# Attention feeding a mixture of experts: the first x sums moved into the last attention batch

## The chip, the cores and the metric

The kernel runs on one core of a Trainium2 chip, as one program. The metric is the time of one execution on the device in microseconds (us); the time before is 684.04 us, the median of three runs from 683.57 to 684.36. The core has five engines that run side by side, each through its own list of instructions in order: PE (TensorE, matrix products; PEld is its weight load), DVE (VectorE), ACT (ScalarE), POOL (GpSimd) and SP (SyncE, which here only issues DMAs). An instruction starts when the one in front of it on its engine is done and when the semaphores it waits for are set.

## What is computed

The output of an attention over sorted blocks is the input of a mixture of eight experts. Cut to what matters here:

```
# attention: batch 4, 8 heads, 768 tokens, head size 64, 8 blocks of 96 tokens
P = five rounds of exp and row and column normalisation of sort_net      # 8 x 8 per head
k_s, v_s = P mixes the blocks of k and of v
x = softmax(q_block . k_s_block / 8) . v_s_block       # -> 3072 tokens x 512

# experts
P = exp(x @ w_gate - max)                              # 3072 x 8
for _ in range(8):
    P /= P.sum(1) + 1e-9; P /= P.sum(0) + 1e-9; P *= 3072 / 8
out = sum over e of P[:, e] * (relu(x @ w1[e]) @ w2[e])     # w1: 512 x 1024, w2: 1024 x 512
```

The largest entry of the logits is taken over all tokens, and the columns of P are summed over all tokens, so the routing can't start before the attention of the last batch is done.

## The kernel before, in words

**Attention.** The four batches follow each other. Batch 0 runs alone; beside batches 1, 2 and 3 the kernel weaves expert 0 of the batch before (`weave`, L371 to L408; `expert`, L294 to L311). For a pair of heads the steps are: `queries` (transposes), `keys` (L188, sorted keys; DVE copies them out of PSUM as kTs, L201), `scores` (L207, products L215 and Exp on ACT), `mix` (L225, products with the values L232; DVE takes reciprocals, L235, and scales, L236, into og), `turn` (L240, transposes L243 and a copy into xtT, L246). xtT holds x with the 512 features on partitions, as four blocks of 128, for all 3072 tokens. `logits` gives L257 and glog (L261). Expert 0 gives L299 and L306 on PE, relu on ACT (L301) and a copy to osbl on DVE or ACT (L314). In this part PE's results go to eight PSUM banks in turn: PE can write a bank again only when the result that lay in it eight turns before has been read.

Under batch 3 POOL loads w1 of expert 1 (L84), makes its eight sums (`sum_w`, L332), and issues the load of w2 of expert 1 (L89).

**Sums for fewer products.** Experts 1 to 7 multiply 2 x 2 blocks with seven products in place of eight (a Strassen form). That needs sums of blocks of each operand: of w1 (`sum_w`), of w2 (`sum_w2`, L449, eight per expert), of x (`sum_x`, L454 to L460, four per 1024 tokens p = 0, 1, 2; three into xc, one in place into xtT), and of the hidden layer (L570, L620). The four x sums of p = 0 need the tokens of batches 0 and 1 alone. All run on POOL, but the x sums of p = 0 and p = 2, which run on DVE.

**SBUF.** The pools of the attention are closed at L410, and the later pools take their place in the order in which they are opened (L415, L416): mpc, xcp (xc), wq and wcq (weights), htp, fsp, hsp, w2q. A later tile waits for the last use of the attention tiles whose place it takes.

**Routing and the seam.** `balance` (L467 to L502) is a chain of small steps: the largest logit (L475, matmul L476, L478), its negative on all partitions (matmul L480, L482 gneg), Exp on ACT (L483), then eight iterations of three thirds: L489 to L491 on DVE (row sums), L493 and L494 on DVE (scale, column sums), and matmul L496 on PE with L497, L499 and L500 on DVE. Each next step hangs on the one in front. Expert 0 of batch 3 (`last_dense`, L669 to L700) is 28 steps of PE: 16 of four matmuls of 128x384 (L687, with a relu on ACT behind each) and 12 of four matmuls of 128x512, half an output tile each (L695, with a copy on ACT behind each second). An order written out by hand, L702 to L704, weaves 13 of these (T), seven steps of the chain (C) and the four x sums (X).

**Rounds.** From L726 a loop of rounds r follows. A round of an expert has seven PE steps p1, p5, p6, p2, p7, p3, p4 (two matmuls of 128x512 each, L519); ACT copies or applies relu behind p1, p5, p6, p2 and p4 (L539, L554, L548, L505); DVE adds and applies relu behind p7 and p3 (L508). Five banks go round: p5 writes the bank that p4 of the round before filled and ACT's relu reads; p4 writes a bank that L508 behind p7 reads. In the first five rounds (r < 5) the loop puts expert 0's last 15 steps between them (`outs`, L746 to L748) and the rest of the chain (L767 to L769). From r = 5 on the rounds carry the output products (L630) of the round five before, and DVE gathers them into osbl (L580).

Nearly all of this is pinned: PE and POOL run in the order of the text. The instructions that are not pinned (the memset and copy at L463 and L465, L314) may be placed among the others by the scheduler.

Of the kernel before, what the change touches and what calls it, by code (L numbers as in the profile page):

```python
# [14 lines left out]
BF16 = mybir.dt.bfloat16  # L15
AF = mybir.ActivationFunctionType
AX = mybir.AxisListType
ALU = mybir.AluOpType


def mkap(t, dims, off=0):
    return bass.AP(tensor=t.tensor, offset=t.offset + off, ap=dims)
# [3 lines left out]
def kernel(  # L26
# [11 lines left out]
    nc = tc.nc  # L38
# [25 lines left out]
    pin = tc.keep_in_program_order  # L64
# [27 lines left out]
    Ibig = ones.tile([128, 128], BF16)  # L92
# [287 lines left out]
    with ExitStack() as c2:  # L380
# [31 lines left out]

    late = lambda name, bufs: ctx.enter_context(
        tc.tile_pool(name=name, bufs=bufs, reuse_waits="tile"))
    mpc, xcp, wq, wcq = late("mpc", 1), late("xcp", 1), late("wq", 2), late("wcq", 1)  # L415
    htp, fsp, hsp, w2q = late("htp", 1), late("fsp", 1), late("hsp", 3), late("w2q", 1)  # L416
    banks = lambda name, bufs: tc.tile_pool(name=name, bufs=bufs, space=bass.MemoryType.PSUM,
                                            reuse_waits="tile")
    load_w2(1)
# [31 lines left out]

    xc = xcp.tile([128, 3, 2, N // 2], BF16)

    def sum_x(p, eng):  # L454
        ta, tb = (slice(1024 * p + 512 * i, 1024 * p + 512 * i + 512) for i in range(2))
        b11, b12, b21, b22 = (xtT[:, k:k + 2, t] for k in (0, 2) for t in (ta, tb))
        x1, x2, x4 = (xc[:, j, :, 512 * p:512 * p + 512] for j in range(3))
        for a, b, c in ((b12, b11, x1), (b22, x1, x2), (b22, b12, b12), (b21, x2, x4)):
            pin(eng.tensor_tensor(out=c, in0=a, in1=b, op=ALU.subtract))
            yield  # L460

    onesc = mpc.tile([128, 128], F32)
    nc.vector.memset(onesc, 1.0)  # L463
    I128 = mpc.tile([128, 128], F32)
    nc.vector.tensor_copy(I128, Ibig)  # L465

    def balance():  # L467

        room = rings["oacc"][2]
        G = room[:, 0:NT * E].rearrange("p (t e) -> p t e", e=E)  # L470
        sums = room[:, 192:192 + NT]
        csps = room[:, 256:256 + E]
        gmps = room[:, 384:512]
        gm = mpc.tile([128, 1], F32)
        pin(nc.vector.reduce_max(out=gm, in_=glog.rearrange("p t e -> p (t e)"), axis=AX.X))  # L475
        pin(nc.tensor.matmul(gmps[0:1, :], gm, I128, start=True, stop=True))  # L476
        gm1 = mpc.tile([1, 1], F32)
        pin(nc.vector.reduce_max(out=gm1, in_=gmps[0:1, :], axis=AX.X, negate=True))  # L478
        yield
        pin(nc.tensor.matmul(csps[:, 0:1], onesc[0:1, :], gm1, start=True, stop=True))  # L480
        gneg = mpc.tile([128, 1], F32)
        pin(nc.vector.tensor_copy(gneg, csps[:, 0:1]))  # L482
        pin(nc.scalar.activation(out=G, in_=glog, func=AF.Exp, bias=gneg))  # L483
        rs2 = mpc.tile([128, NT], F32)
        cs2 = mpc.tile([128, E], F32)
        cs1 = mpc.tile([128, E], F32)
        yield
        for it in range(8):
            pin(nc.vector.reduce_sum(out=sums, in_=G, axis=AX.X))  # L489
            pin(nc.vector.tensor_scalar_add(rs2, sums, 1e-9))  # L490
            pin(nc.vector.reciprocal(out=rs2, in_=rs2))  # L491
            yield
            pin(nc.vector.tensor_mul(G, G, mkap(rs2, [rs2.ap[0], rs2.ap[1], [0, E]])))  # L493
            pin(nc.vector.reduce_sum(out=cs2, in_=G.rearrange("p t e -> p e t"), axis=AX.X))  # L494
            yield
            pin(nc.tensor.matmul(csps, onesc, cs2, start=True, stop=True))  # L496
            pin(nc.vector.tensor_scalar(out=cs1, in0=csps, scalar1=float(E) / N,  # L497
                                        scalar2=1e-9 * E / N, op0=ALU.mult, op1=ALU.add))
            pin(nc.vector.reciprocal(out=cs1, in_=cs1))  # L499
            pin(nc.vector.tensor_mul(glog if it == 7 else G, G,  # L500
                                     mkap(cs1, [cs1.ap[0], [0, NT], cs1.ap[1]])))
            yield  # L502
# [166 lines left out]
    def last_dense():  # L669

        at = [0]

        def two_banks():
            at[0] += 1
            return rings["oacc"][at[0] % 2]

        for c in range(2):
            c0 = (B - 1) * S + c * 384
            if c == 0:
                h = [hTb[1][:, fb, 0:384] for fb in range(8)]  # L680
            else:
                two = [hsp.tile([128, 4, 384], BF16, name="hs") for _ in range(2)]
                h = [two[fb // 4][:, fb % 4, :] for fb in range(8)]
            for fb in range(8):
                hps = (rings["bk"][(0, 2, 3)[fb % 3]] if c == 0 else two_banks())[:, 0:384]
                for kk in range(4):
                    pin(nc.tensor.matmul(hps, w1t[0][:, kk, fb * 128:(fb + 1) * 128],  # L687
                                         xtT[:, kk, c0:c0 + 384],
                                         start=(kk == 0), stop=(kk == 3)))
                pin(relu(h[fb], hps))  # L690
                yield
            for tt in range(3):
                oacc = rings["bk"][(1, 4)[tt]] if c == 0 and tt < 2 else two_banks()
                for fb in range(8):
                    pin(nc.tensor.matmul(oacc, h[fb][:, tt * 128:(tt + 1) * 128],  # L695
                                         w2t[0][:, fb, :], start=(fb == 0), stop=(fb == 7)))
                    if fb == 3:
                        yield
                pin(nc.scalar.copy(osbl[:, c0 // 128 + tt, :], oacc))
                yield  # L700

    dense, chain, xs = last_dense(), balance(), sum_x(0, nc.vector)  # L702
    for step in "TTCXTTXCXXTTCCTTTCCTTCTT":
        next({"T": dense, "C": chain, "X": xs}[step])  # L704

    queue = [sum_w2(1), sum_x(1, nc.gpsimd)]

    def weights(n):
# [6 lines left out]
    C = 3 * (E - 1)  # L715
# [4 lines left out]
    for m, o in enumerate(ends):  # L720
        e, p, hT, _ = chunks[-1]
        for j in range(2):
            spares += plain(e, p, 4 * j + o.i, hT, bank, 2 if m == 1 and j == 1 else 1)
    late, before = None, None
    weights(8)
    for r in range(len(pairs) + 6):  # L726
        n, i = r // 4, r % 4
        if n < C:
            e, p, hT, s3 = chunks[n]
            if i == 0 and (n == 1 or n > 1 and p == 0) and e + 1 < E:  # L730
                load_w1(e + 1)
                queue.append(sum_w(e + 1))
            if r == 8 or p == 1 and i == 2 and n > 1 and e + 1 < E:
                load_w2(2 if r == 8 else e + 1)
                queue.append(sum_w2(2 if r == 8 else e + 1))
            steps, rest = hidden(e, p, i, hT, s3, r < 4)
        else:
            steps, spares, rest = spares[:7], spares[7:], None
        if r == 5:
            xs = sum_x(2, nc.vector)  # L740
        k = r - 5
        if k + 1 in range(len(pairs)):
            pairs[k + 1].sums()
        weights((0, 2, 2, 0, 0)[r] if r < 5 else 4 if r < 8 else 1 + i % 2)
        now = pairs[k] if k in range(len(pairs)) else None
        if r < 5:  # L746
            outs = [None, lambda: next(dense), None, lambda: next(dense), None,
                    lambda: next(dense)]  # L748
        else:
            outs = [getattr(a, b) for a, b in  # L750
                    ((now, "q5"), (before, "q7"), (now, "q1"), (before, "q4"),
                     (now, "q6"), (now, "q2"), (now, "q3")) if a]
        if r == 5:
            for _ in chain:
                pass
            scale0([0, 4])
        for j in range(max(len(steps), len(outs))):
            if j < len(steps):
                steps[j]()
                if j == 3 and n < C:  # L760
                    if k + 1 in range(1, 12):
                        scale0([8 * ((k + 1) // 4) + (k + 1) % 4 + 4 * m for m in range(2)])
                    if k + 1 in range(len(pairs)):
                        pairs[k + 1].keep()
            if j < len(outs) and outs[j]:
                outs[j]()
            if r < 5 and j in (0, 1, 3, 4, 5):  # L767
                if (5 * r + (0, 1, 0, 2, 3, 4)[j]) % 4 != 3:
                    next(chain, 0)  # L769
            if j == 1 and late:  # L770
                late()
                late = None
            if j == 3:
                next(xs, 0)
        late, before = rest, now
        if n >= C and not spares and not before:
            break
# [30 lines left out]
```

## Time and profile before

| | |
|---|---|
| runs | 683.57, 684.04, 684.36 us |
| profiled execution, its own time | 683.67 us |
| its span, first to last instruction | 681.9 us |
| granted clock of PE, mean | 0.999 |
| PE busy in 130 to 140 and in 140 to 150 us | 9.32 and 7.13 of 10 |
| PE busy in 240 to 300 us | 59.58 of 60 |
| first L687 step of the seam | 134.44 us |
| first L519 step (round 0) | 148.87 us |
| first step of round 5 | 177.83 us |
| one x sum (128x1024) on DVE | 0.68 to 1.66 us |
| one x sum on POOL | 2.12 us |
| one w1 or w2 sum (128x512) on POOL | 1.14 to 1.61 us |
| w2 load of an expert (1 MB), issue to landing | 9.0 us |

The profile is one execution. A row of a timeline has the start in us, the time in us, the engine, the line, the operation, what is written and read with its size, how many instructions were merged, and in square brackets how long the engine was idle in front and what ended that. Matmuls are pipelined and their ends are modelled: two rows of PE can overlap, and the distance from one start to the next tells more than the time of one. A row of the waits has the engine, the tile and line that waited, what it waited for, the sum, how often, and the longest.

### The profile page before, as it was taken

How to read it: one execution, taken by the hardware profiler on the slowest of the kernel's cores; microseconds unless marked ns; L12 is line 12 of the kernel's file. 1: busy time of each engine (PE TensorE's matmuls, PEld its weight loads, DVE VectorE, ACT ScalarE, POOL GpSimd, SP SyncE). 2: the span in 40 equal slices, each digit the busy share in tenths (PEclk: the TensorE clock that was granted, in tenths of full speed). 3: DMA queues.
4: the chain of work that ended last, by engine and by line, in shares of the span. 5: the costliest groups of instructions: out<-in, count | busy, mean ns of one | idle time of the engine just before them, and what ended most of it. 6: DMA issues, size and time to landing. Idle time of an engine off the chain costs nothing.

```text
span 681.9 us, 13271 instructions
## 1 busy us (share of the span) xinstructions
PE 655.4 (96%) x5058; PEld 434.1 (64%) x5136; DVE 475.6 (70%) x979; ACT 379.6 (56%) x736; POOL 473.8 (69%) x437
## 2 busy tenths in 40 slices
PE   5989999989999999999999999999999999999997
PEld 2646666544566666666666666666666666666665
DVE  6627555676687777777777777777777777777775
ACT  3746646347677765555555555555555555555540
POOL 4542323574888998949698987879796979836641
PEclk9999999999999999999999999999999999999999
DMA  9898843400221304030303021030403040000224
GB/s 147 161 214 131 136 87 63 62 1 10 53 46 18 62 1 63 1 62 1 62 2 58 4 39 26 4 59 1 62 1 62 1 62 1 1 0 32 93 81 169
DMA packets 31905, 36.58 MB, mean 54 GB/s; under 512 B 2016, under 2 KB 24288, under 8 KB 31840
## 3 DMA queue, kind: packets, MB, share of 16 engines
q0 software_dynamic: 26400, 27.82, 25.3%
q1 hardware_dynamic: 5440, 7.90, 3.4%
q8 instruction: 40, 0.66, 0.4%
q14 instruction: 25, 0.20, 0.1%
HBM read 52.45 MB, written 6.29 MB: 86 GB/s over the span
## 4 chain that ended last, share of the span: by engine, by line
PE 82%; DMA 7%; POOL 5%; DVE 4%; issue 1%; ACT 1%; SPq 0%; DVEq 0%; POOLq 0%; ACTq 0%
PE oacc L630 34%; PE bk L519 32%; PE bank L306 4%; PE bank L299 4%; DMA qt<-in_q_dram 3%; POOL hs L620 3%; DMA w2e<-in_moe_w_dram 1%; PE bank L232 1%; DMA w1e<-in_moe_w_dram 1%; PE bk L596 1%; POOL wc L332 1%; PE oacc L695 1%; DMA vsb<-vs 1%; PE bank L215 1%; PE oacc L687 1%
## 5 line engine op out<-in xcount | busy, mean ns | idle before, releaser
L580 DVE SCALAR_TENSOR_TENSOR osbl<-oacc,glog,osbl 128x256 f32<-128x256 f32 (+1 forms) x410 | 219.3, 535 | 127.3 <-PE oacc L630 117.2
L505 ACT ACTIVATE hT<-bk 128x512 bf16<-128x512 f32 (+1 forms) x176 | 104.1, 593 | 148.0 <-PE bk L519 129.8
L519 PE MATMUL bk<-xtT,w1e 128*128 128x512 bf16 x478 | 144.3, 379 | 0.9
L630 PEld LDWEIGHTS <-hs 128*128 128x128 bf16 x984 | 96.2, 98 | 63.0 <-issue 0.3
L630 PEld LDWEIGHTS <-hT 128*128 128x128 bf16 x904 | 88.4, 98 | 59.6 <-issue 2.4
L620 POOL TENSOR_TENSOR hs<-hT 128x512 bf16<-128x512 bf16 x82 | 94.8, 1157 | 37.7 <-DVE hT L508 32.3
L630 PE MATMUL oacc<-w2e,hT 128*128 128x256 bf16 x764 | 114.6, 273 | 1.6 <-DVE osbl L580 1.1
L620 POOL TENSOR_TENSOR hs<-hT,hs 128x512 bf16<-128x512 bf16 x82 | 95.2, 1161 | 6.4
L620 POOL TENSOR_TENSOR hs<-hs,hT 128x512 bf16<-128x512 bf16 x82 | 95.2, 1161 | 6.4
L519 PE MATMUL bk<-xc,wc 128*128 128x512 bf16 x316 | 95.6, 379 | 0.9 <-ACT hT L505 0.8
L630 PE MATMUL oacc<-w2e,hs 128*128 128x256 bf16 x616 | 92.4, 273 | 0.7
L519 PEld LDWEIGHTS <-w1e 128*128 128x128 bf16 x672 | 65.8, 98 | 12.8 <-issue 1.4
L508 DVE CUSTOM_DVE_ANT_0 hT<-bk,p 128x512 bf16<-128x512 f32 x84 | 58.1, 691 | 9.3 <-PE bk L519 1.8
L554 ACT COPY p<-bk 128x512 f32<-128x512 f32 x84 | 49.2, 586 | 24.0 <-PE bk L519 21.3
L548 ACT COPY u<-bk 128x512 f32<-128x512 f32 x84 | 49.3, 586 | 23.0 <-PE bk L519 20.3
L539 ACT COPY bk<-bk 128x512 f32<-128x512 f32 x84 | 48.0, 571 | 20.5 <-PE bk L519 20.5
L508 DVE CUSTOM_DVE_ANT_0 hT<-bk,u 128x512 bf16<-128x512 f32 x84 | 57.1, 680 | 0.0
L630 PE MATMUL oacc<-w2s,hs 128*128 128x256 bf16 x368 | 55.2, 273 | 0.3
L519 PEld LDWEIGHTS <-wc 128*128 128x128 bf16 x504 | 49.3, 98 | 9.2 <-issue 1.6
L573 DVE SCALAR_TENSOR_TENSOR s<-bk,hT 128x512 bf16<-128x512 f32 x80 | 54.5, 681 | 0.0
L519 PE MATMUL bk<-xtT,wc 128*128 128x512 bf16 x160 | 48.2, 379 | 0.4
L519 PE MATMUL bk<-xc,w1e 128*128 128x512 bf16 x159 | 48.0, 379 | 0.4 <-DVE hT L508 0.3
(128 smaller groups left out, 857.0 us busy)
## 6 DMA issues: line engine op xcount, KB each, us to landing
w1e<-in_moe_w_dram POOLq DMA_DIRECT2D x8, 1024.0 KB, 8.1
w2e<-in_moe_w_dram POOLq DMA_DIRECT2D x8, 1024.0 KB, 9.0
out_dram<-osbl SPq DMA_DIRECT2D x23, 256.0 KB, 2.0
vt<-in_v_dram POOLq DMA_DIRECT2D x3, 768.0 KB, 10.8
vsb<-vs SPq DMA_DIRECT2D x16, 97.5 KB, 5.2
vsb<-vs POOLq DMA_DIRECT2D x16, 97.5 KB, 5.2
qt<-in_q_dram POOLq DMA_DIRECT2D x4, 384.0 KB, 13.2
kt<-in_k_dram POOLq DMA_DIRECT2D x4, 384.0 KB, 13.8
```

Source lines behind the costliest of these rows:

```text
L299: hold(nc.tensor.matmul(hps[:, 0:n], w1t[e][:, kk, fb * 128:(fb + 1) * 128], xtT[:, kk, c0:c0 + n], start=(kk == 0), stop=(kk == 3)))
L306: hold(nc.tensor.matmul(oacc, hTs[:, fb, tt * 128:(tt + 1) * 128], w2t[e][:, fb, :], start=(fb == 0), stop=(fb == 7)))
L505: relu = lambda o, x: nc.scalar.activation(out=o, in_=x, func=AF.Relu)
L508: return nc.vector._custom_dve(TENSOR_ADD_SAT, out=o, in0=x, in1=y, s0=TOP, s1=0.0)
L519: pin(nc.tensor.matmul(ps, wa[:, kk, :], xa[:, kk, :], start=(first and kk == 0), stop=(kk == 1), skip_group_check=True))
L539: pin(nc.scalar.copy(t["w"], t["u"]))
L548: pin(nc.scalar.copy(t["u2"], t["u"]))
L554: pin(nc.scalar.copy(t["p5"], t["v"]))
L573: pin(nc.vector.scalar_tensor_tensor(out=s3[:, i, :], in0=t["w"], scalar=0.0, in1=c12, op0=ALU.max, op1=ALU.subtract))
L580: pin(nc.vector.scalar_tensor_tensor(out=o, in0=ps, scalar=glog[:, t, e:e + 1], in1=o, op0=ALU.mult, op1=ALU.add))
L620: pin(nc.gpsimd.tensor_tensor(out=s[:, c], in0=a, in1=b, op=o))
L630: pin(nc.tensor.matmul(ps, h[:, fb, :], w[:, fb, :], start=(first and fb == 0), stop=(fb == 3), skip_group_check=True))
```

## The change

The four x sums of p = 0 are moved from the seam to where the later pools are opened, without being pinned, so the scheduler may place them as soon as their tiles allow. The pools fsp and hsp are opened first, which puts xc over the key and value buffers of the attention. `sum_x` takes the function that pins as an argument.

A tiny copy on POOL, first_x, reads the last of these sums, and it is pinned in POOL's order after the w1 sums; since the load of w2 of expert 1 (`load_w2(1)`) and its sums stand behind it on POOL, these come after the x sums. In the built order DVE has three x sums right after the last kTs copy of batch 3, in front of an osbl copy (L314) and of the mix of the second head pair, and the fourth after the next osbl copy; POOL has memset, first_x, the w2 load, then the w2 sums, then its own x sums for p = 1, as before.

The memset of onesc goes from DVE to POOL and the copy I128 from DVE to ACT. In the built order DVE's L475 stands right behind glog and in front of the last osbl copy.

The order of the seam has the same 13 T and seven C: T stands in pairs between the C's at first. In the rounds r < 5 expert 0's steps stand after p1, p6 and p7 in place of p5, p2 and p3, and a third of the chain is issued in three of each four of all six places, where before it was three of four in five places. The 19 thirds that are left end with the first place of round 4.

```diff
@@ -412,8 +412,9 @@
+    hsp, fsp = late("hsp", 3), late("fsp", 1)
     mpc, xcp, wq, wcq = late("mpc", 1), late("xcp", 1), late("wq", 2), late("wcq", 1)
-    htp, fsp, hsp, w2q = late("htp", 1), late("fsp", 1), late("hsp", 3), late("w2q", 1)
+    htp, w2q = late("htp", 1), late("w2q", 1)
@@ -451,18 +452,22 @@
-    def sum_x(p, eng):
+    def sum_x(p, eng, hold=pin):
...
-            pin(eng.tensor_tensor(out=c, in0=a, in1=b, op=ALU.subtract))
+            hold(eng.tensor_tensor(out=c, in0=a, in1=b, op=ALU.subtract))
...
-    nc.vector.memset(onesc, 1.0)
+    nc.gpsimd.memset(onesc, 1.0)
     I128 = mpc.tile([128, 128], F32)
-    nc.vector.tensor_copy(I128, Ibig)
+    nc.scalar.copy(I128, Ibig)
+    for _ in sum_x(0, nc.vector, lambda ins: ins):
+        pass
+    first_x = mpc.tile([128, 2], BF16)
+    pin(nc.gpsimd.tensor_copy(first_x, xc[:, 2, 0, 0:2]))
@@ -699,9 +704,9 @@
-    dense, chain, xs = last_dense(), balance(), sum_x(0, nc.vector)
-    for step in "TTCXTTXCXXTTCCTTTCCTTCTT":
-        next({"T": dense, "C": chain, "X": xs}[step])
+    dense, chain, xs = last_dense(), balance(), iter(())
+    for step in "TTCTTCTTCCTTCCTTTCTT":
+        next({"T": dense, "C": chain}[step])
@@ -744,7 +749,7 @@
-            outs = [None, lambda: next(dense), None, lambda: next(dense), None,
+            outs = [lambda: next(dense), None, lambda: next(dense), None,
                     lambda: next(dense)]
@@ -764,9 +769,8 @@
-            if r < 5 and j in (0, 1, 3, 4, 5):
-                if (5 * r + (0, 1, 0, 2, 3, 4)[j]) % 4 != 3:
-                    next(chain, 0)
+            if r < 5 and j < 6 and (6 * r + j) % 4 != 3:
+                next(chain, 0)
```

## Prediction

> **What bounds the kernel now.** I read the page's busy times first, then the waits of PE, then the timelines of PE, DVE and POOL around the change, and for the changed program the built order of each engine's instructions with the semaphores they wait for. Lines are those of the kernel before (behind L457 the changed file counts five more).
>
> ```profile
> PE 655.4 (96%) x5058; PEld 434.1 (64%) x5136; DVE 475.6 (70%) x979; ACT 379.6 (56%) x736; POOL 473.8 (69%) x437
> ```
>
> PE is the bound: it is idle for 26.5 us in all. What a change between the attention and the experts can win is PE time at that seam. PE's waits between 136 and 146 us:
>
> ```profile
> PE oacc L496 <- DVE cs L494: 2.1, 1, 2.1
> PE bk L687 <- ACT hT L505: 0.7, 1, 0.7
> PE oacc L476 <- DVE gm L475: 0.6, 1, 0.6
> ```
>
> The same in PE's timeline; L687 and L695 are expert 0's last steps, L476, L480 and L496 the routing's matmuls, 148.87 the first of expert 1:
>
> ```profile
> 136.54 0.38 PE L476 MATMUL oacc<-I,gm 128*1 128x128 f32 x2 [0.63 <-DVE gm L475]
> ...
> 141.43 0.81 PE L687 MATMUL bk<-xtT,w1e 128*128 128x384 bf16 x4 [0.74 <-ACT hT L505]
> ...
> 145.18 0.39 PE L496 MATMUL oacc<-cs,onesc 128*128 128x8 f32 x2 [2.08 <-DVE cs L494]
> ...
> 148.87 0.59 PE L519 MATMUL bk<-xtT,w1e 128*128 128x512 bf16 x2
> ```
>
> DVE shows why: four x sums (L459) lie among the routing's small steps; gneg waits behind two, the first third (L489) behind four.
>
> ```profile
> 137.16 1.66 DVE L459 TENSOR_TENSOR xc<-xtT 128x1024 bf16<-128x1024 bf16 x1
> 138.85 1.53 DVE L459 TENSOR_TENSOR xc<-xtT,xc 128x1024 bf16<-128x1024 bf16 x1
> 140.31 0.14 DVE L482 COPY gneg<-oacc 128x1 f32<-128x1 f32 x1
> 140.37 1.56 DVE L459 TENSOR_TENSOR xtT<-xtT 128x1024 bf16<-128x1024 bf16 x1
> 141.86 1.64 DVE L459 TENSOR_TENSOR xc<-xtT,xc 128x1024 bf16<-128x1024 bf16 x1
> 143.42 0.35 DVE L489 TENSOR_REDUCE oacc<-oacc 128x24 f32<-128x192 f32 x1
> ```
>
> POOL runs its w2 sums beside them; alone one takes 1.15:
>
> ```profile
> 137.12 1.15 POOL L449 TENSOR_TENSOR w2s<-w2e,w2s 128x512 bf16<-128x512 bf16 x1
> 138.23 1.60 POOL L449 TENSOR_TENSOR w2s<-w2e 128x512 bf16<-128x512 bf16 x1
> ```
>
> The two take turns: each x sum ends some 0.55 after a POOL sum does, each POOL sum about 1.0 after an x sum. One that starts just as a POOL sum ends takes 0.68 (195.32 us), and it is the next POOL sum that stretches, to 1.63. Three in a row cost 141.93 - 137.16 = 4.77.
>
> **The change, part by part.**
>
> *Seam: what goes.* From starts, not modelled ends: L687's eight matmuls take 1.30, so L476 could have started at 135.74 and lost 0.80; L480 lost 0.10 (138.15 to 138.25); the last L687 step 0.93 (140.50 to 141.43); L496 2.24 (142.94 to 145.18). Sum 4.07: without waits expert 1 starts at 144.80. Do other waits come instead? In the new order gm stands right behind glog on DVE (133.57), the memset goes to POOL, the I128 copy (0.74 on DVE) to ACT, where 1.82 us lie idle at 114 us; gm is there by 133.95, L476 needs it at 135.74. gm1 (0.41 behind L476) is ready by 136.45, its matmul stands two steps later, at 137.35. gneg follows at 137.9, Exp (0.42) ends at 138.46, the first thirds (0.95 for L489 to L491, 0.76 for L493 and L494) end at 140.2; PE has eight steps done by then, at 140.25. No wait is left: gain 4.07.
>
> *Attention: what comes.* The new layout puts xc over key and value buffers; the program's semaphores ask only for loads long landed and for ACT's xtT copies of batches 0 and 1. So sums 1 to 3 start as soon as DVE has copied the last keys (kTs, 116.72), and stand in front of the osbl copy L314. There POOL runs the w1 sums L332 without a gap, which nothing holds:
>
> ```profile
> 116.75 1.16 POOL L332 TENSOR_TENSOR wc<-wc,w1e 128x512 bf16<-128x512 bf16 x1
> ...
> 124.63 0.94 POOL L89 DMA_DIRECT2D w2e<-in_moe_w_dram  x1
> ```
>
> This is the same neighbour as at 137 us, so I take the same 4.77: from 116.85 to 121.6. DVE's next steps and PE's in the kernel before:
>
> ```profile
> 117.84 0.69 DVE L314 COPY osbl<-bank 128x512 f32<-128x512 f32 x1 [1.12 <-PE bank L306]
> 118.44 0.24 DVE L235 RECIPROCAL recips<-bank 96x4 f32<-96x4 f32 x2
> ```
> ```profile
> 121.16 0.56 PE L215 MATMUL bank<-qTs,kTs 64*96 64x96 bf16 x16
> 121.65 1.47 PE L299 MATMUL bank<-xtT,w1e 128*128 128x384 bf16 x8
> ```
>
> The first is DVE, the second PE. PE's eight banks go round: the program's L215 needs the bank that this L314 empties, and the L299 behind it the bank of the last L236 of the same mix. L314 at 121.6 instead of 117.84 ends at 122.3, so L215 waits 1.2; that L236 ends 2.43 behind L314's start (120.27 - 117.84), at 124.03, so L299 starts at 124.08 instead of 121.65. Cost 2.43. Every later bank that I followed (L232, L243, L306) is free in time, by 0.2 us or more, and the delay stays 2.43. Sum 4 stands in an idle stretch (1.99 before 123.33) and ends near 126.4, ahead of what PE needs. Bounds for the three sums: 3 x 0.60 and the rest of one POOL sum, 2.9 (PE loses 0.6), and POOL never giving way (below). I take the alternation, the nearest row.
>
> *POOL and queues.* The w1 sums end 1.2 later (125.9), then memset, first_x waiting for sum 4, and w2's DMA: issued at 126.6 instead of 124.63, landed after its 9.0 at 135.6. Behind first_x only that load and the w2 sums queue: 8 x 1.15 without DVE's turns to 144.8, POOL's own x sums to 149.1 (148.8 before). The next user is POOL's s sum, which waits for a DVE result at 153.6: 4.5 us of cover, which also hides the memset, 0 to 2 us. SP's queue is untouched.
>
> *The five rounds (r < 5).* Before: starts 148.87 and 177.83, 28.96. Inside, p5 waits for ACT's relu of the round before:
>
> ```profile
> 154.33 0.59 PE L519 MATMUL bk<-xtT,w1e 128*128 128x512 bf16 x2
> 155.18 0.59 PE L519 MATMUL bk<-xc,wc 128*128 128x512 bf16 x2 [0.25 <-ACT hT L505]
> ```
>
> p1 to p5 is 0.85 instead of 0.43: 0.42 lost here, the same in rounds 2 and 3, 0.28 in round 4, 0.12 before a p4: 1.66. Expert 0's step (0.65 or 0.86) now stands between p1 and p5 and covers the relu. New are the denser thirds: 19 of them over 25 slots. I replayed the rounds by the rows: thirds 0.95, 0.76, 0.85; relu sum L508 0.60 and p4 0.73 behind its start; L519 pair 0.43. In rounds 1 and 3 two thirds stand in front of the L508 that p4 needs. Round 1 from its p1: DVE still has an L508 (0.19 to 0.79) and two thirds (to 2.50); the matmul of the next third stands at 2.60, the third runs from 2.92 to 3.77, one more to 4.72; then L508, so p4 can start at 5.45 and was due at 4.68: 0.77. Round 3 the same way: thirds from 3.35 to 4.20 and 5.15, p4 at 5.88, due at 5.33: 0.55. Elsewhere DVE is ahead. So 28.96 - 1.66 + 1.32 = 28.6: gain 0.3. The chain ends 3 us earlier, which pays nothing: ACT's scale0 after it starts right behind a relu (178.03 to 178.63), not behind glog (178.38), so the 1.12 wait at 180.42 stays.
>
> *Sum.* 4.07 - 2.43 + 0.3 = 1.95. From round 5 on the instructions are the same and PE sets the pace (59.5 to 59.6 busy in every 60 us), so the gain stays. Span 681.9 to 679.95; with the 1.77 around it 683.67 to 681.7. The profiled run lies 0.37 under the median, so for a median 682.1.
>
> **A rule against the trace.** The rows: 1.53 to 1.66 beside POOL, 0.68 at 195.32. The Trainium skill (SBUF — State Buffer, Who interferes with whom) says that VectorE with two SBUF inputs and a GpSimd instruction that reads SBUF lock each other out, and that the order of issue decides who blocks. By it the change runs into the unheld w1 sums, as the rows say too; but if DVE's queued sums were issued ahead of POOL's next one, POOL would stand and the three cost the 2.9 of the first rival.
>
> **Rivals.**
> 1. *Cheap sums.* DVE keeps the port: L314 at 119.8, PE loses 0.6, gain 3.8: 680.2. For: the 0.68 and 0.97 rows. Against: all four turns at 137 us. Chance 0.14.
> 2. *The thirds bind DVE.* If p4 waits in all five rounds by the mean 0.66, 3.3 instead of 1.32, the gain is gone: 684.1. For: two rounds do already. Against: 16.2 of thirds and some 6 of L508 in 28.6 us. Chance 0.20.
> 3. *Slower: POOL never gives way.* If DVE gets the port only when the w1 sums end at 124.7, L314 comes at 126.5, 4.9 later than I say, and each microsecond of it is one of PE: 687.0. It decides from L314 later than 123.5. Against: the turns at 137 us. Chance 0.12.
>
> **Numbers.** My forecast has 0.54; its own range is 681 to 683.1. A measurement here tells 0.2%, 1.4 us: under 682.7 is faster, over 685.4 slower. Of the forecast 0.48 is faster and 0.06 the same; rival 1 is faster; of rival 2 0.16 the same and 0.04 slower; rival 3 slower: 0.62, 0.22, 0.16. From rival 1 to past rival 2 is 680.0 to 685.0, which leaves out rival 3 and a tail below.
>
> **What would show it.** Right: three L459 of 1.5 to 1.7 on DVE at 117 to 121.6, PE waiting at L215 and L299 for DVE for 2.4 in sum, no PE wait over 0.2 at L476 and L496 (new L481, L501), w2 sums of 1.15, p5 without a wait, two p4 waits of 0.5 to 0.8, round 5 near 175.9. Wrong: x sums of 0.7 (rival 1), p4 waits in every round (2), an L314 past 123.5 (3), or PE waits behind round 5 that were not there.

## The result, and the profile after

The changed kernel takes 681.35 us, the median of six runs (680.58 to 681.98), against 683.77 for the kernel before in the same comparison: a ratio of 0.9957, 95% interval 0.9946 to 0.9969. The forecast was 682.1, with a range of 680.0 to 685.0; the measured time is 0.75 under it. The profiled execution of the changed kernel took 680.97, its span is 679.2 us, 2.70 under the span before.

Where the 2.70 came from is read from starts of PE instructions. Four marks cut the span: the L299 step in front of the second L215 group of batch 3, the first step of `last_dense` (L687 before, L692 after), the first step of round 0 (L519, L524), and the first step of round 5.

| us | start of that L299 | attention, to last_dense | seam, to round 0 | rounds 0 to 4 | round 5 to the end |
|---|---|---|---|---|---|
| before | 120.42 | 14.02 | 14.43 | 28.96 | 504.07 |
| after | 119.58 | 15.83 | 10.57 | 28.61 | 504.61 |
| gain | 0.84 | -1.81 | 3.86 | 0.35 | -0.54 |

Spans are printed to 0.1 us, so the last column, and what is worked out from it below, is good to some 0.05.

The 0.84 in front is no gain of the change: over the fourteen profiled kernels of this document that start lies anywhere from 119.58 to 120.69, with PE's waits for the first loads; PE has the 0.84 already at 57 us. So the sums below go by the time from that L299 to the end, which holds the change and not the start: 561.48 before, 559.62 after, a gain of 1.86.

Busy times of the page of the kernel after: PE is the bound as before.

```profile
PE 659.0 (97%) x5136; PEld 434.1 (64%) x5136; DVE 474.8 (70%) x977; ACT 380.5 (56%) x737; POOL 473.6 (70%) x439
```

PE's timeline at the seam, kernel after. L481, L485 and L501 are the matmuls that were L476, L480 and L496:

```profile
135.41 1.46 PE L692 MATMUL bk<-xtT,w1e 128*128 128x384 bf16 x8
136.81 0.38 PE L481 MATMUL oacc<-I,gm 128*1 128x128 f32 x2
137.12 1.47 PE L692 MATMUL bk<-xtT,w1e 128*128 128x384 bf16 x8
138.52 0.38 PE L485 MATMUL oacc<-gm,onesc 1*128 1x1 f32 x2
138.83 2.77 PE L692 MATMUL bk<-xtT,w1e 128*128 128x384 bf16 x16
141.44 0.36 PE L501 MATMUL oacc<-cs,onesc 128*128 128x8 f32 x2
```

No square bracket stands behind any of them: the three matmuls of the routing find their operands ready, and the 2.08, 0.74 and 0.63 that stood here before are gone.

What was paid for it lies 20 us earlier. DVE's timeline, then POOL's, kernel after (L460 are the x sums, L332 the w1 sums):

```profile
114.83 1.05 DVE L201 CAST kTs<-bank 128x384 bf16<-128x384 f32 x2
115.77 1.32 DVE L460 TENSOR_TENSOR xc<-xtT 128x1024 bf16<-128x1024 bf16 x1
117.20 1.46 DVE L460 TENSOR_TENSOR xc<-xtT,xc 128x1024 bf16<-128x1024 bf16 x1
118.57 1.64 DVE L460 TENSOR_TENSOR xtT<-xtT 128x1024 bf16<-128x1024 bf16 x1
120.14 0.68 DVE L314 COPY osbl<-bank 128x512 f32<-128x512 f32 x1
```
```profile
115.39 1.15 POOL L332 TENSOR_TENSOR wc<-wc,w1e 128x512 bf16<-128x512 bf16 x1
116.50 1.60 POOL L332 TENSOR_TENSOR w1e<-w1e 128x512 bf16<-128x512 bf16 x1
118.06 1.60 POOL L332 TENSOR_TENSOR wc<-w1e,wc 128x512 bf16<-128x512 bf16 x1
...
125.19 0.20 POOL L464 MEMSET onesc<- 128x128 f32 x1
125.33 0.18 POOL L470 COPY first_x<-xc 128x2 bf16<-128x2 bf16 x1
125.46 0.94 POOL L89 DMA_DIRECT2D w2e<-in_moe_w_dram  x1
```

The two take turns, as at 137 us in the kernel before: each x sum ends some 0.55 to 0.6 behind a POOL sum, and each POOL sum stretches from 1.15 to 1.60. PE pays in front of L215, in its timeline:

```profile
119.58 0.81 PE L299 MATMUL bank<-xtT,w1e 128*128 128x384 bf16 x4
120.87 0.20 PE L215 MATMUL bank<-qTs,kTs 64*96 64x96 bf16 x1 [0.48 <-DVE osbl L314]
121.41 0.57 PE L215 MATMUL bank<-qTs,kTs 64*96 64x96 bf16 x8 [0.34 <-DVE og L236]
122.29 0.38 PE L215 MATMUL bank<-qTs,kTs 64*96 64x96 bf16 x7 [0.30 <-DVE og L236]
122.62 1.47 PE L299 MATMUL bank<-xtT,w1e 128*128 128x384 bf16 x8
```

Finally, two waits of PE behind round 5's start that the forecast did not have, in the timeline of the kernel after (p4 of rounds 5 and 6). Before, round 5 had none and round 6 one of 0.34.

```profile
181.55 0.59 PE L524 MATMUL bk<-xc,w1e 128*128 128x512 bf16 x2 [0.56 <-DVE hT L513]
187.79 0.59 PE L524 MATMUL bk<-xc,w1e 128*128 128x512 bf16 x2 [0.44 <-DVE hT L513]
```

### The profile page after: what moved, and what is told of

Same layout as the page of the kernel before. It is cut to its first block, busy times and chain, and to the rows that moved or that the text cites. A ratio compares the mean times of both kernels' runs of the same rounds, so it can differ in the third digit from the quotient of the medians.

```text
span 679.2 us, 13352 instructions
## 1 busy us (share of the span) xinstructions
PE 659.0 (97%) x5136; PEld 434.1 (64%) x5136; DVE 474.8 (70%) x977; ACT 380.5 (56%) x737; POOL 473.6 (70%) x439
## 4 chain that ended last, share of the span: by engine, by line
PE 88%; DVE 5%; DMA 4%; issue 1%; ACT 1%; POOL 1%; SPq 0%; DVEq 0%; POOLq 0%
PE oacc L635 36%; PE bk L524 36%; PE bank L299 4%; PE bank L306 3%; DMA qt<-in_q_dram 3%; PE bank L232 1%; PE bk L601 1%; PE oacc L700 1%; PE bk L692 1%; DMA vsb<-vs 1%; PE bank L215 1%; PE bank L196 1%; PE bank L243 1%; DVE xc L460 1%; PE bk L700 1%
## 5 line engine op out<-in xcount | busy, mean ns | idle before, releaser
L524 PE MATMUL bk<-xtT,w1e 128*128 128x512 bf16 x504 | 149.1, 379 | 0.0
L524 PE MATMUL bk<-xc,wc 128*128 128x512 bf16 x336 | 99.1, 379 | 0.0
L524 PEld LDWEIGHTS <-w1e 128*128 128x128 bf16 x672 | 65.7, 98 | 14.9 <-issue 3.6
L524 PEld LDWEIGHTS <-wc 128*128 128x128 bf16 x504 | 49.4, 99 | 7.5
L524 PE MATMUL bk<-xc,w1e 128*128 128x512 bf16 x168 | 49.9, 379 | 1.9 <-DVE hT L513 1.8
L524 PE MATMUL bk<-xtT,wc 128*128 128x512 bf16 x168 | 50.0, 379 | 0.0
## 6 DMA issues: line engine op xcount, KB each, us to landing
vt<-in_v_dram POOLq DMA_DIRECT2D x3, 768.0 KB, 10.5
```

The lines of the kernel that those rows point to most:

```text
L524: pin(nc.tensor.matmul(ps, wa[:, kk, :], xa[:, kk, :], start=(first and kk == 0), stop=(kk == 1), skip_group_check=True))
```

## The experiments

The theory after the result:

- (a) the moved x sums carry the gain, by freeing the seam;
- (b) their price in the attention is DVE taking turns with POOL's w1 sums, nothing else;
- (c) first_x holds nothing;
- (d) the denser thirds cost what the new places of expert 0's steps win;
- (e) the loss behind round 5 is the x sums of p = 2 meeting POOL's sums at another moment.

The rival to (b) is the place itself, three sums in front of an osbl copy; the rival to (a) is that the new order and the rounds carry the gain; the rival to (e) is that something of the rounds' end reaches over into round 5.

The last three columns are stages of the profiled execution, by starts. The kernels e1 to e4, e5 to e7 and e8 to e10 ran on one chip each, e11 on one of its own and e12 on that of e5 to e7, always beside runs of the kernel before of that chip, to which the ratio goes.

| kernel | median, us | ratio to before, 95% | attention | rounds 0 to 4 | L299 to end |
|---|---|---|---|---|---|
| before | 683.77 | | 14.02 | 28.96 | 561.48 |
| after | 681.35 | 0.9957 (0.9946, 0.9969) | 15.83 | 28.61 | 559.62 |
| e1_no_hold | 681.23 | 0.9959 (0.9944, 0.9975) | 15.47 | 28.60 | 559.19 |
| e2_w1_held | 679.95 | 0.9940 (0.9927, 0.9952) | 14.03 | 28.61 | 557.79 |
| e3_move_only | 680.62 | 0.9951 (0.9939, 0.9964) | 15.82 | 28.96 | 559.13 |
| e4_old_thirds | 679.91 | 0.9941 (0.9928, 0.9953) | 15.70 | 27.74 | 558.18 |
| e5_scale_early | 680.78 | 0.9955 (0.9941, 0.9970) | 15.74 | 28.61 | 559.13 |
| e6_held_old_thirds | 678.33 | 0.9917 (0.9903, 0.9932) | 14.03 | 27.75 | 556.58 |
| e7_held_even_thirds | 678.58 | 0.9921 (0.9906, 0.9937) | 14.02 | 28.17 | 556.88 |
| e8_sums_behind | 680.06 | 0.9953 (0.9941, 0.9965) | 15.76 | 28.61 | 558.61 |
| e9_best | 678.57 | 0.9932 (0.9920, 0.9945) | 14.03 | 28.17 | 556.84 |
| e10_phase | 680.19 | 0.9956 (0.9944, 0.9969) | 15.78 | 28.60 | 558.46 |
| e11_best4 | 678.80 | 0.9923 (0.9909, 0.9937) | 14.03 | 28.17 | 556.59 |
| e12_load_early | 678.25 | 0.9915 (0.9899, 0.9930) | 14.03 | 28.17 | 556.27 |

The interval of a ratio is some 0.8 us either way, so steps of less than that are read from the traces, one of each kernel, not from the medians. From the first step of round 12 to the end all fourteen traces take 459.7 to 459.9, so what is left to scatter there is small. In every one of these but the kernel before, the seam takes 10.5 to 10.6.

### e1_no_hold: without first_x

```diff
-    first_x = mpc.tile([128, 2], BF16)
-    pin(nc.gpsimd.tensor_copy(first_x, xc[:, 2, 0, 0:2]))
```

> The changed kernel without first_x, so nothing holds the w2 load and the w2 sums. My theory: first_x costs and gains nothing, because in the changed kernel's profile the fourth x sum ends at 124.23 and the w1 sums in front of first_x on POOL only at 125.2; the w2 load is issued at most 0.3 earlier, the three x sums keep their 4.4 us, the time stays within 0.4 us of 681.35. Rival (the hold keeps the w2 sums off the x sums): x sums of 1.5 now in the fourth place too, PE's waits in the attention grow by 1 us or more, time 682.5 or more.

Measured: 681.23, the changed kernel's 681.35 within its scatter. In the trace of the changed kernel the fourth x sum runs from 123.55 to 124.23, and POOL's last w1 sum ends at 125.2, so first_x waits for nothing. The hold is without effect, because what runs beside the x sums is not the w2 sums behind it but the w1 sums in front of it.

### e2_w1_held: POOL's w1 sums behind the x sums

```diff
-                for _ in sums:
-                    pass
+                pass
...
     pin(nc.gpsimd.tensor_copy(first_x, xc[:, 2, 0, 0:2]))
+    for _ in sums:
+        pass
```

> The changed kernel with the w1 sums also behind first_x, so POOL is quiet while DVE makes the x sums. My theory (POOL's w1 sums make the x sums slow, and their delay goes into PE through the banks): the three x sums take 0.68 each, 1.9 in sum instead of 4.4, the osbl copy behind them comes some 1.9 us after the last kTs copy, PE waits for DVE at L215 for less than 0.3 us instead of 1.1 in three waits, the way from the L299 in front to the first L692 shrinks from 15.8 to 14.1 us, and the time falls by 1.5 to 1.8 us to some 679.7. POOL's work is pushed back by 6 us: its s sums start 3 us late and catch up before round 5. Rival 1 (the DVE time of the sums itself is the cost, not the neighbour): as the changed kernel, 681.3. Rival 2 (POOL is too late afterwards): attention faster but PE waits for POOL's sums in rounds 4 to 7, time 681.3 or more.

Measured: 679.95; the attention is back to 14.03 (14.02 before). DVE's timeline of this run, where POOL stands still:

```profile
116.72 0.67 DVE L459 TENSOR_TENSOR xc<-xtT 128x1024 bf16<-128x1024 bf16 x1
117.49 0.69 DVE L459 TENSOR_TENSOR xc<-xtT,xc 128x1024 bf16<-128x1024 bf16 x1
118.10 0.68 DVE L459 TENSOR_TENSOR xtT<-xtT 128x1024 bf16<-128x1024 bf16 x1
118.70 0.68 DVE L314 COPY osbl<-bank 128x512 f32<-128x512 f32 x1
```

The place is the same, three sums in front of L314, and L314 starts 1.98 behind the first of them instead of 4.37; PE then waits for neither osbl nor og. So the 1.80 of the attention is the turns with POOL alone, and the place by itself costs nothing. The w1 sums start at 123.00 in place of 114.17 and run undisturbed to 132.2, 7 us later than in the changed kernel, and are still in time: the seam and the rounds take as long as there.

### e3_move_only: the x sums moved, the order of the seam and the rounds as before

```diff
-    for step in "TTCTTCTTCCTTCCTTTCTT":
+    for step in "TTCTTCTTCCTTTCCTTCTT":
...
-            outs = [lambda: next(dense), None, lambda: next(dense), None,
+            outs = [None, lambda: next(dense), None, lambda: next(dense), None,
...
-            if r < 5 and j < 6 and (6 * r + j) % 4 != 3:
-                next(chain, 0)
+            if r < 5 and j in (0, 1, 3, 4, 5):
+                if (5 * r + (0, 1, 0, 2, 3, 4)[j]) % 4 != 3:
+                    next(chain, 0)
```

The order of the seam is that of the kernel before with the X's taken out. The layout, the hold, the memset on POOL and the I128 copy on ACT are those of the changed kernel.

> The x sums, layout, hold, memset and copy as changed, but the seam's order and the rounds as before (the order without its X, expert 0's steps behind p5, p2 and p3, thirds in three of four of five places). My theory: the move alone carries the seam's gain (first L692 to round 0 in 10.5 to 10.9 us), the rounds give back 0.3 (28.9 instead of 28.6 us), time 681.7. Rival (the order and the rounds carry the gain): the seam's wait at the third's matmul stays at 1 us or more, or the rounds take 29.5 or more, time 683 or more.

Measured: 680.62, and 559.13 against 559.62 by the trace: no slower than the whole change, where a loss against it was expected. The seam takes 10.48 with the old order, so the new order of T and C wins nothing. The rounds are 0.35 longer, as expected, but from round 5 to the end it takes 503.87 where the changed kernel takes 504.61. The expectation had carried over the forecast's "from round 5 on the same", which is the step that failed here too. So neither the new order nor the rounds carry the gain: the rival to (a) is refuted. The x sums are not alone in it, though: e3 has the memset, the I128 copy and L475 in their new places too, and a part of the seam's gain is theirs by the rows (under the seam, below).

### e4_old_thirds: new places for expert 0's steps, old places for the thirds

```diff
-            if r < 5 and j < 6 and (6 * r + j) % 4 != 3:
-                next(chain, 0)
+            if r < 5 and j in (0, 1, 3, 4, 5):
+                if (5 * r + (0, 1, 0, 2, 3, 4)[j]) % 4 != 3:
+                    next(chain, 0)
```

> The changed kernel with the thirds of the chain in three of four of five places of a round, as before; expert 0's steps stay behind p1, p6 and p7. My theory: the denser thirds only make p4 wait for DVE (1.3 us in all in rounds 0 to 3 of the changed kernel) and end the chain 3 us too early; with the old thirds these waits fall to 0.3 or less, the rounds take 27.6 to 27.9 us instead of 28.6, ACT's scale0 in round 5 still starts right behind its relu, time 680.4. Rival (the denser thirds are needed): the chain ends after round 5 has begun, scale0 waits for glog, PE's wait in round 5 grows from 1.1 to 2 us or more, time 681.5 to 682.5.

Measured: 679.91. The rounds take 27.74: against e3 (28.96) the new places win 1.22, and against the changed kernel (28.61) the denser thirds cost 0.87. A piece of the expectation missed: the scaling of osbl (`scale0`) did not stay right behind its relu, for with the chain ending later it waits for glog, and PE's wait in round 5 grows from 1.12 to 1.60 (PE's timeline of this run):

```profile
176.99 0.60 PE L635 MATMUL oacc<-w2e,hT 128*128 128x256 bf16 x4 [1.60 <-DVE osbl L585]
```

So an earlier end of the chain is worth 0.48, and it cost 0.87.

### e5_scale_early: the scaling a round earlier

```diff
-            scale0([0, 4])
         for j in range(max(len(steps), len(outs))):
...
+            if r == 4 and j == 3:
+                scale0([0, 4])
```

> The changed kernel with ACT's first scaling of expert 0's output (scale0([0, 4])) issued in round 4, behind its fourth place, in place of the start of round 5; the chain has ended by then. Theory: round 5's output step waits 1.12 for osbl only because that scaling stands at the head of round 5, not because the chain is late; issued a round earlier it is done, the wait goes, and the time is 1.1 under the changed kernel: 680.2. Rival: ACT is full there, the relu or copies behind it come later, and PE waits as long at p4 or p5 of round 4: no gain, 681.3.

Measured: 680.78, 559.13 by the trace. The wait in round 5 fell from 1.12 to 0.19, as the theory had it, but a gain of 1.1 did not come: 0.5 by the trace, and neither expectation names the reason. DVE's timeline, POOL's and PE's of this run, in round 7:

```profile
191.49 1.66 DVE L460 TENSOR_TENSOR xtT<-xtT 128x1024 bf16<-128x1024 bf16 x1
```
```profile
191.45 1.16 POOL L625 TENSOR_TENSOR hs<-hT 128x512 bf16<-128x512 bf16 x1
192.68 1.48 POOL L625 TENSOR_TENSOR hs<-hs,hT 128x512 bf16<-128x512 bf16 x1
```
```profile
193.80 0.59 PE L524 MATMUL bk<-xc,w1e 128*128 128x512 bf16 x2 [1.02 <-DVE hT L513]
```

POOL's sum began 0.04 ahead of the x sum. That x sum took 1.66, and the relu sum behind it, which p4 needs, came a microsecond late. In the changed kernel the same x sum began 0.07 ahead of POOL's (192.73 and 192.80) and took 0.68.

### e6_held_old_thirds: e2 and e4 together

The edits are those two.

> The changed kernel with the w1 sums of POOL behind the x sums (as in e2_w1_held) and with the thirds at the old five places (as in e4_old_thirds). Theory: the two repairs lie in different stages and add up: attention 14.0, rounds 27.7, round 5 still waits about 1.6 for the scaling; time 1.35 + 1.35 under the changed kernel, 678.5 by the two medians. Rival: what one gains the other loses again behind round 5, where the x sums of p = 2 meet POOL's sums in another phase: 679.5 or more.

Measured: 678.33, by the theory's 678.5: the two add up. By the trace it is 3.04 under the changed kernel (1.83 from e2, 1.44 from e4, sum 3.27). The x sums of rounds 5 and 6 take 0.81 and 0.82 here.

### e7_held_even_thirds: e2, evenly spread thirds, the scaling in round 4

```diff
-            scale0([0, 4])
...
-            if r < 5 and j < 6 and (6 * r + j) % 4 != 3:
-                next(chain, 0)
+            if r < 5 and j < 6 and (j != 2 or r in (0, 2)):
+                places += 1
+                if places % 4:
+                    next(chain, 0)
+            if r == 4 and j == 4:
+                scale0([0, 4])
```

The w1 sums are held as in e2, and `places` starts at 0.

> The changed kernel with the w1 sums held, the thirds spread as evenly as the old five places but with one place more in rounds 0 and 2, so that the chain ends in round 4, and scale0([0, 4]) issued in round 4 behind its fifth place. Theory: attention 14.0, rounds 28.0 or less, no wait for osbl in round 5: the parts add up to 677.0. Rival: the added places bring the p4 waits back, or the scaling delays a relu in round 4: 678 or more.

Measured: 678.58, the rival's side. The rounds take 28.17, not under 28.0. The wait of 1.6 for osbl is gone, and PE's timeline shows two others: 0.66 in round 5 for ACT's relu, which the scaling delays, and 1.01 in round 7 for the relu sum behind an x sum that POOL was 0.05 ahead of (189.51 and 189.56).

```profile
174.46 0.59 PE L525 MATMUL bk<-xc,wc 128*128 128x512 bf16 x2 [0.66 <-ACT hT L511]
...
191.87 0.59 PE L525 MATMUL bk<-xc,w1e 128*128 128x512 bf16 x2 [1.01 <-DVE hT L514]
```

### e10_phase: work added to POOL

To e5, which has that wait of 1.02, two tiny memsets are added on POOL.

```diff
         k = r - 5
+        if r == 7:
+            for _ in range(2):
+                pin(nc.gpsimd.memset(first_x, 0.0))
```

> e5_scale_early with two tiny memsets (128x2) on POOL at the head of round 7, in front of its sums: they add work of some 0.3 and change nothing else. Theory: the x sum of round 7 took 1.66 in e5 because POOL's sum had started 0.04 ahead of it (191.45 and 191.49); pushed behind, POOL starts second, the x sum takes 0.68 and POOL's sum stretches instead, p4's wait of 0.97 goes, and added work makes the kernel 1.0 faster: 679.8. Rival: who starts first does not matter, or POOL's later sums pay it back: 680.8 or more.

DVE's timeline of this run, then POOL's:

```profile
192.30 0.68 DVE L460 TENSOR_TENSOR xtT<-xtT 128x1024 bf16<-128x1024 bf16 x1
```
```profile
192.24 0.26 POOL L749 MEMSET first_x<- 128x2 bf16 x2
192.45 1.55 POOL L625 TENSOR_TENSOR hs<-hT 128x512 bf16<-128x512 bf16 x1
```

Now starting 0.15 behind, POOL's sum is the one that stretches, the x sum takes 0.68, and PE's wait at p4 of round 7 is gone: from round 0's start that p4 comes at 46.76 instead of 47.73. That shows the mechanism of (e): who starts first decides, a shift of 0.2 turned it round, and the difference is one microsecond of PE. The time: 680.19, between the theory's 679.8 and the rival's 680.8; by the trace 0.67 under e5, of the 0.97 won in round 7. The ratios to the kernel before (0.9956, and 0.9955 for e5) don't show this; their intervals are wider than it. The other 0.30 of the trace went in round 10, on which e11 bears. The Trainium skill (SBUF — State Buffer, Who interferes with whom) calls the port that VectorE's second SBUF input shares with GpSimd an exclusive lock, kept for the whole instruction by the one that issued first. These two pairs of rows agree with it. The printed starts tell the order only down to some 0.03, as the fourth x sum in the timelines of the kernel after shows, DVE's and then POOL's:

```profile
123.55 0.68 DVE L460 TENSOR_TENSOR xc<-xtT,xc 128x1024 bf16<-128x1024 bf16 x1
```
```profile
123.52 1.72 POOL L332 TENSOR_TENSOR wc<-w1e,wc 128x512 bf16<-128x512 bf16 x1
```

Here POOL's sum has the earlier start, by 0.03, and is all the same the one that stretches. With 0.04 it held DVE, in e5 and at 137.12 in the kernel before.

### e8_sums_behind: the x sums of p = 2 behind the relu sums

On e5:

```diff
-            if j == 3:
+            if j == (3 if r == 8 else 5):
                 next(xs, 0)
```

> e5_scale_early with the x sums of p = 2 on DVE issued two places later in rounds 5, 6 and 7, behind the second relu sum in place of in front of the first; the fourth, in round 8, stays. Theory: in e5 PE loses 0.25, 0.29 and 0.97 at p4 in rounds 5, 6 and 7 (by starts), because a long x sum stands in front of the relu sum that p4 needs; behind it the sums delay nothing urgent, so 1.5 goes: 679.3. Rival: DVE is as tight there, the sums then delay the output steps' gathers, and PE waits for a bank of the outputs instead: 680.8 or more.

Measured: 680.06, and 0.52 under e5 by the trace instead of 1.5. The waits at p4 in rounds 5, 6 and 7 are all gone, so they hung on the place of the x sums, and the rival to (e) falls. But the fourth x sum, left where it was, now meets POOL badly (PE waits 0.77 at p4 of round 8), and in round 10 PE waits 0.52 for POOL.

### e9_best and e11_best4: the same in the fastest form

e9 puts e8's edit on e7 and takes the two scalings apart; e11 also starts the x sums a round earlier.

```diff
         if r == 5:
             for _ in chain:
                 pass
+            scale0([4])
...
-            if r == 4 and j == 4:
-                scale0([0, 4])
+            if r == 4 and j == 3:
+                scale0([0])
...
-            if j == 3:
+            if j == (3 if r == 8 else 5):
                 next(xs, 0)
```
```diff
-        if r == 5:
+        if r == 4:
             xs = sum_x(2, nc.vector)
...
-            if j == (3 if r == 8 else 5):
+            if j == 5:
```

> e7_held_even_thirds with the x sums of p = 2 issued two places later in rounds 5 to 7 (as in e8_sums_behind), and with the two scalings of scale0 apart: the one of block 0 in round 4 behind the fourth place, the one of block 4 at the head of round 5 as in the changed kernel. Theory: the p4 wait of 1.0 in round 7 goes and the wait of 0.66 for ACT's relu in round 5 falls to 0.3 or less: 678.6 - 1.0 - 0.4 = 677.2. Rival: as for e8_sums_behind, 678.5 or more.

> e9_best with the four x sums of p = 2 one round earlier, in rounds 4 to 7, each behind the second relu sum. Theory: in e9 only the fourth, left in round 8 in front of the relu sum, met a POOL sum that had begun ahead of it, and cost PE 0.99; now all four stand where a long one delays nothing urgent: about 1.0 under e9, 677.6. Rival: behind the second relu sum they delay an output step's gather (e9 shows 0.37 of that in round 6), so the metre only moves: 678.4 or more.

Measured: 678.57 and 678.80, neither under e7's 678.58 by more than the scatter. In e9 the fourth x sum costs 0.99 in round 8. In e11 PE waits for no x sum and no relu sum behind round 0 any more. Instead it waits for POOL in round 10. PE's timeline of e11, then POOL's:

```profile
205.55 0.61 PE L636 MATMUL oacc<-w2s,hs 128*128 128x256 bf16 x4 [1.24 <-POOL hs L626]
```
```profile
194.32 0.92 POOL L89 DMA_DIRECT2D w2e<-in_moe_w_dram  x1
...
203.23 1.15 POOL L449 TENSOR_TENSOR w2e<-w2e 128x512 bf16<-128x512 bf16 x1 [4.32 <-DMA w2e<-in_moe_w_dram]
204.34 1.15 POOL L626 TENSOR_TENSOR hs<-hT 128x512 bf16<-128x512 bf16 x1
```

The load of w2 of expert 2 stands on POOL behind the sums of rounds 5 to 7 (seven of 1.15 to 1.6 in each of the first two, over 8 us, where a round of PE takes 6.1, and three in the last), so it is issued late, 2.8 us behind the start of PE's round 8; POOL's first sum of it waits 4.32, and the hidden layer's sum that PE needs stands behind that. In e8 and e10 it is the same sum that PE waits for in round 10, 0.52 and 0.30. Counted from the start of round 0, the p4 of round 10 comes at 65.68 in e8, 65.49 in e10 and 65.34 in e11 (66.52 in the changed kernel), although their p4 of round 9 came at 58.91, 59.11 and 57.85: what e11 had won up to there, POOL took back. e6 comes to 65.32 without waiting for POOL, by waiting 1.60 in round 5 where the others don't.

### e12_load_early: that load two rounds earlier

On e11:

```diff
+            if r == 6:
+                load_w2(2)
             if r == 8 or p == 1 and i == 2 and n > 1 and e + 1 < E:
-                load_w2(2 if r == 8 else e + 1)
+                if r > 8:
+                    load_w2(e + 1)
                 queue.append(sum_w2(2 if r == 8 else e + 1))
```

> e11_best4 with the load of w2 of expert 2 issued by POOL at the head of round 6 in place of round 8; its sums stay where they were. Theory: with the waits at p4 gone, PE reached round 10 earlier than POOL, whose first w2 sum stood 4.32 for that load and held the hidden layer's sums behind it, so PE waited 1.24 there and the gain of the moved x sums was given back; with the load landed before, this wait goes: 678.8 - 1.2 = 677.6. Rival: POOL is behind by its own work in rounds 5 to 8, and the issue of 0.92 two rounds earlier only makes the sums of rounds 6 and 7 late: 678.5 or more.

Measured: 678.25, between the two. The wait of 4.32 on POOL and PE's 1.24 in round 10 are gone (p4 there at 65.04), and PE waits 0.94 in round 8 for POOL's hs instead:

```profile
192.61 0.61 PE L636 MATMUL oacc<-w2s,hs 128*128 128x256 bf16 x4 [0.94 <-POOL hs L626]
```

Both are true: the load was the wall, and POOL's own work is the next, 0.3 further on. It is the fastest of all by the trace (556.27) and by the median, but its medians and e6's (678.33) cannot be told from each other. e6 is the version to keep: two small edits, some 3 us under the changed kernel, and 0.9917 of the kernel before.

## Why the prediction was right, and which step was wrong

**The seam: 4.07 forecast, 3.86 measured.** Right, by its own steps: no wait at L481, L485 or L501. e3 adds what the forecast had not separated: the old order does as well (10.48). What L476 lost was not the x sums' doing. DVE's timeline of the kernel before:

```profile
134.64 0.69 DVE L314 COPY osbl<-bank 128x512 f32<-128x512 f32 x1 [1.07 <-PE bank L306]
135.31 0.17 DVE L463 MEMSET onesc<- 128x128 f32 x1
135.39 0.74 DVE L465 CAST I<-Ibig 128x128 f32<-128x128 bf16 x1
136.05 0.34 DVE L475 TENSOR_REDUCE gm<-glog 128x1 f32<-128x192 f32 x1
```

The first x sum starts behind all that, at 137.16. In the kernel after, gm's step starts at 134.58, and L481 loses 0.10 where L476 lost 0.80. So by these rows 0.7 of the 3.86 comes from moving the memset, the I128 copy and L475, and some 3.2 from the x sums; no run has the one without the other. The 0.21 that is missing from 4.07 is 0.10 each at L481 and L485.

**The attention: -2.43 forecast, -1.81 measured.** The mechanism was right to the letter, x sums taking turns with the unheld w1 sums, PE in front of L215 and L299 paying for it; e2 shows that nothing else is in it. The size was off in one term: L314 was put 4.88 behind the end of the kTs copy and came 4.26 behind it (120.14 - 115.88). The first x sum met a POOL sum already under way (115.39) and ended at 117.09, where the forecast had charged a full turn for it: the three sums took 4.37 in place of 4.77, and the first started 0.11 ahead of that copy's end in place of 0.13 behind it. The 0.62 that L314 came earlier is the 0.62 that PE lost less. Rivals 1 (cheap sums, 680.2) and 3 (POOL never gives way, 687.0) fell with the same rows: turns of 1.32, 1.46 and 1.64.

**POOL behind it.** The w1 sums ended at 125.2 and the load went at 125.46, against 125.9 and 126.6: earlier by the same turn and by the start of the whole execution, and first_x, put down as a possible wait, found its sum ready. The cover of 4.5 us was not touched.

**The rounds: 0.3 forecast, 0.35 measured.** The sum of p4's waits came out as forecast, 1.32 by starts, but in other places: 0.34, 0.60 and 0.38 in rounds 0, 1 and 3 against 0.77 and 0.55 in rounds 1 and 3; the equal sum is luck. Rival 2 (every round, 684.1) did not come. e4 shows what the forecast never asked: the denser thirds, which the change needs for an earlier end of the chain, cost 0.87 of the 1.22 that the new places win. The forecast had 1.32 and 1.66 for these two (the wait in round 0 is there with the old thirds too), so both terms were some 0.45 too large, and that their difference came out right is luck.

**"From round 5 on the instructions are the same and PE sets the pace, so the gain stays".** This step failed, by 0.54: rounds 5 and 6 take 14.06 in place of 13.41, and 0.1 of the difference comes back later. The instructions are the same, but they do not meet the same neighbours. DVE's x sum in round 5 starts 4.67 behind that round's start in the changed kernel and 4.66 in e3; POOL's sums started 3.37 behind it in the one and 2.68 in the other. In the changed kernel that put a POOL sum 0.07 ahead of the x sum. Two rows, DVE's and POOL's timelines of the kernel after, then the same two of the kernel before:

```profile
179.26 1.64 DVE L460 TENSOR_TENSOR xc<-xtT 128x1024 bf16<-128x1024 bf16 x1
```
```profile
179.19 1.15 POOL L332 TENSOR_TENSOR wc<-wc,w1e 128x512 bf16<-128x512 bf16 x1
```
```profile
182.50 0.97 DVE L459 TENSOR_TENSOR xc<-xtT 128x1024 bf16<-128x1024 bf16 x1
```
```profile
181.77 1.16 POOL L332 TENSOR_TENSOR wc<-wc,w1e 128x512 bf16<-128x512 bf16 x1
```

The sum takes 1.64 where it took 0.97 before, and p4 of that round waits 0.56, that of the next 0.44. e10 shows the mechanism by itself, in round 7. What sets POOL's 0.69 between the changed kernel and e3 was not traced further than to the hidden layer's sums in front.

**The total.** By stages: 3.86 - 1.81 + 0.35 - 0.54 = 1.86 against 1.95 (the forecast's three terms as printed add to 1.94). Two misses, 0.62 too much cost in the attention and 0.54 too little behind round 5, nearly cancel, and the seam's 0.21 with them, so that the sum comes within 0.1 is luck; what was right is the mechanism of the seam and of the attention. By the medians the gain is 2.42, and the ratio's interval is 2.1 to 3.7, so 1.86 lies just outside it; the start in front of the first mark differs by up to 1.1 between executions, and what part it has in the median can't be seen from one profile each.

## What to carry to other kernels

When work is moved to a place where its engine is idle, look at what the neighbour on the shared port is doing there, and hold that neighbour, not the one behind it: here the hold stood one step too late, and moving the right sums behind it was worth 1.8 us. Never count a later stage as unchanged because its instructions are: where two engines run strings of such sums side by side, 0.1 to 0.2 us of shift decides which one stretches, so put a sum that may stretch behind, not in front of, the result that PE waits for. And before squeezing waits one by one, find the next deadline (here a load that POOL issued late): three different repairs ended within 0.4 us of each other at the same wall.

## What the runs showed that was not expected

- The time of one and the same x sum follows from the moment at which it starts: 0.68 when DVE is ahead of POOL by 0.07, 1.64 when it is behind by 0.07; between them it is the rest of the running POOL sum and some 0.55 (0.81 with 0.27 left in e6, 0.97 with 0.43 left before). Within 0.03 the printed starts don't tell: in seven of the traces the fourth x sum of p = 0 starts 0.02 to 0.03 behind a POOL sum and takes 0.68.
- Added work made a kernel faster: two memsets of 0.26 in sum on POOL took 0.67 off the time from L299 to the end, by one trace of each kernel; the ratios are too coarse to show it.
- In strict turns both lose: three x sums cost DVE 4.4 instead of 2.0, and POOL's w1 sums beside them take 1.60 instead of 1.15.
